# Spreading the last stores over two queues, reordering the last two chunks, and filling an early gap of VectorE, in an attention and mixture-of-experts kernel

## The chip, the cores and the metric

The kernel runs on one core of one Trainium2 chip. The metric is the device time of one execution in microseconds (us), taken as the median of several runs. The profile's span, from the first to the last instruction, is about 1.7 to 1.8 us shorter than the device time of the same run.

## The reference

Four batches and eight heads of causal attention (768 positions, 64 columns a head). Three of the eight heads see everything before them, the others only four first positions and a window of 64. The result, 3072 tokens of 512 columns, goes through eight experts whose gate weights are normalised eight times over rows and columns.

```python
def _moe_ref(x, w_gate, w1, w2):          # x: 3072 x 512 from the attention
    P = np.exp(logits - logits.max())     # logits = x @ w_gate, 8 experts
    for _ in range(8):
        P /= P.sum(1, keepdims=True) + 1e-09
        P /= P.sum(0, keepdims=True) + 1e-09
        P *= N / E
    out = np.zeros((N, D), dtype=np.float32)
    for e in range(E):
        h = np.maximum(x @ w1[e], 0.0)    # 512 -> 1024
        out += P[:, e:e + 1] * (h @ w2[e])  # 1024 -> 512
    return out
```

## The kernel before

The attention and the gate take the first 175 us. Then come 42 work items, seven experts times six chunks of 512 tokens. Each runs a first layer and a second layer, both with seven block products in place of eight, which needs sums and differences of blocks ("combinations") made on VectorE beforehand. The chunks' accumulators are named acc_79 to acc_84 in the profile. In the last expert each finished quarter of an accumulator is stored at once. The parts that matter (all else cut):

```python
works = [(e, c) for e in range(1, E) for c in range(NCH)]     # 7 experts x 6 chunks

def store(c, i, n):                       # a quarter of a chunk: two transfers of 128 KB
    for o in range(2):
        nc.sync.dma_start(                # all of them issued by SyncE
            out=out[ts(c, CH), :].rearrange(...)[i, n, o],
            in_=acc[c][64 * o:64 * o + 64, i, n, :, :])

def layer2(e, c):                         # 7 products: l2y, l2w, l2z in the profile
    ...
    for k in (1, 5, 6, 2, 7, 3, 4):
        bank, first, last, (i, n) = steps[k]
        product(k, bank, first, last)     # TensorE
        add(bank, i, n, by_dma=k in (...) and (e, c) not in works[-2:])
        ...                               # VectorE, or ScalarE and an accumulating DMA
        if e == E - 1 and done[i, n] == (1 if (i, n) == (1, 0) else 2):
            store(c, i, n)
        yield

def layer2_last(e, c):                    # the very last chunk: plain, "last" in the profile
    for q, i in ((0, 0), (0, 1), (1, 0), (1, 1)):
        ...                               # 8 matmuls of 512 columns, VectorE adds to acc
                for o in range(2):
                    (nc.scalar if o else nc.sync).dma_start(out=..., in_=acc[c][...])
                yield

# when VectorE makes which combination: (work item, slot) -> w2 ("w") or x ("x")
early = {(1, 1): "w", (1, 4): "xx", (2, 0): "w", (2, 1): "x", (2, 3): "w", (2, 4): "x",
         (3, 1): "wx", (3, 4): "x", (3, 5): "wx", (4, 1): "wx", (4, 5): "w"}

def body(n):
    ...
    if n == 0:
        run(gens["l1"], 9); run(combine_w1(1), 9); run(combine_x(0), 9)
        gens["w"], gens["x"] = combine_w2(1), combine_x(1)
        go("w")
        weigh_over()
    ...

with tc.manual_schedule(engines={mybir.EngineType.DVE}):      # VectorE's order is the program's
    for n in range(len(works)):
        body(n)
    go("h", 2)
    last = layer2_last(*works[-1])
    run(last, 1)                          # the last chunk's first block ...
    go("l2", 9)                           # ... then layer 2 of the chunk before it
    run(last, 9)
```

In this stage VectorE runs in program order. The orders of the other engines come from a scheduler.

The softmax here doesn't subtract the row's maximum and nothing guards it: scores larger than these inputs give would overflow.

Of the kernel before, what the change touches and what calls it, by code (L numbers as in the profile page):

```python
# [37 lines left out]
def kernel(  # L38
# [13 lines left out]
    nc = tc.nc  # L52
# [3 lines left out]
    E = moe_w_gate.shape[1]  # L56
# [93 lines left out]
    def load_w1(e):  # L150
        w1 = wp.tile([128, 4, FF], F16, tag="w1", name=f"w1_{e}")
        nc.gpsimd.dma_start(out=w1, in_=moe_w1[e].rearrange("(c p) f -> p c f", p=128))  # L152
        return w1

    def load_w2(e):
        w2 = wp.tile([128, 8, DM], F16, tag="w2", name=f"w2_{e}")
        nc.gpsimd.dma_start(out=w2, in_=moe_w2[e].rearrange("(c p) f -> p c f", p=128))
        return w2
# [246 lines left out]
    def run(g, n):  # L405
        for _ in range(n):
            if next(g, "end") == "end":
                return False
        return True
# [250 lines left out]
    def weigh_over():  # L660
        nc.vector.reciprocal(out=over0[:, :, 0], in_=Pne[:, :, 0])
        nc.vector.tensor_tensor(
            out=over0[:, :, 1:], in0=Pne[:, :, 1:LATE],
            in1=over0[:, :, 0:1].broadcast_to([128, NB, LATE - 1]), op=ALU.mult)
# [4 lines left out]
    def weight_first(c):  # L669


        wt = mp.tile([128, 4], F32, tag="wt", name=f"wt_{c}")

        def hold(i0, i1):
            nc.vector.tensor_copy(out=wt[:, i0:i1], in_=Pne[:, 4 * c + i0:4 * c + i1, 0])

        def weigh(i0, i1):
            for i in range(i0, i1):
                x = acc_of(4 * c + i)
                nc.scalar.activation(out=x, in_=x, func=AF.Copy, bias=0.0, scale=wt[:, i:i + 1])  # L680

        hold(0, 1)
        yield
        weigh(0, 1)
        yield
        hold(1, 4)
        yield
        weigh(1, 4)
        yield

    works = [(e, c) for e in range(1, E) for c in range(NCH)]
# [23 lines left out]
    def combine_w1(e):  # L715
        w1 = expw[e][0]
        X = mp.tile([128, 4, 2, 2, 256], F16, tag="S1", name=f"S1_{e}")
        w1 = w1.rearrange("p c (h i x) -> p c h i x", h=2, i=2)
        yield from left(lefts1, e, [[w1[:, 2 * k:2 * k + 2, :, i, :] for k in range(2)]
                                    for i in range(2)], [X[:, j] for j in range(4)])  # L720

    def combine_w2(e):
        w2 = expw[e][1]
        X = mp.tile([128, 4, 4, 256], F16, tag="T2", name=f"T2_{e}")
        yield from right(rights2, e, [[w2[:, 4 * k:4 * k + 4, ts(n, 256)] for n in range(2)]
                                      for k in range(2)], [X[:, j] for j in range(4)])

    def combine_w(e):
        yield from combine_w1(e)
        yield from combine_w2(e)  # L730

    def combine_x(d):
        X = mp.tile([128, 4, 2, 512], F16, tag=f"T1_{d}", bufs=1, name=f"T1_{d}")
        yield from right(rights1, d, [[xT[k][:, :, ts(2 * d + n, CH)] for n in range(2)]
                                      for k in range(2)], [X[:, j] for j in range(4)])

    def combine_h(e, c):
        h = [hTs[e, c, k].rearrange("p f (q i t) -> p i q f t", q=2, i=2) for k in range(2)]
        X = [mp.tile([128, 2, 4, 128], F16, tag=f"S2{j}", bufs=1, name=f"S2{j}_{e}_{c}")
             for j in range(4)]  # L740
        yield from left(lefts2, (e, c), [[h[k][:, i] for k in range(2)] for i in range(2)], X)
# [86 lines left out]

    def store(c, i, n):
        for o in range(2):  # L830
            nc.sync.dma_start(
                out=out[ts(c, CH), :].rearrange("(q i p c) (n d) -> i n c p q d", q=2, i=2, c=2, n=2)[i, n, o],
                in_=acc[c][64 * o:64 * o + 64, i, n, :, :],
            )

    def layer2(e, c):
# [39 lines left out]
        for k in (1, 5, 6, 2, 7, 3, 4):  # L876
            bank, first, last, (i, n) = steps[k]
            product(k, bank, first, last)
            add(bank, i, n, k in ((2, 3, 4, 7) if (e, c) in works[:2] else (2, 3, 4))
                and (e, c) not in works[-2:])  # L880
            done[i, n] = done.get((i, n), 0) + 1
# [4 lines that stand above are left out]
    def layer2_last(e, c):  # L886


        w2 = expw[e][1]
        for q, i in ((0, 0), (0, 1), (1, 0), (1, 1)):  # L890
            pieces = 1 + (q == 1 and i == 1)
            for n in range(pieces):
                width = 512 // pieces
                t = psB.tile([128, 512], F32, tag="l1" if n else "l2", name=f"last{q}{i}{n}")
                t = t[:, 0:width]
                for f in range(8):
                    nc.tensor.matmul(out=t, lhsT=hTs[e, c, f // 4][:, f % 4, ts(2 * q + i, 128)],  # L897
                                     rhs=w2[:, f, n * width:(n + 1) * width],
                                     start=(f == 0), stop=(f == 7))
                cols = slice(n, n + 1) if pieces == 2 else slice(0, 2)  # L900
                dst = acc[c][:, i, cols, q, :]
                nc.vector.scalar_tensor_tensor(
                    out=dst, in0=t.rearrange("p (n d) -> p n d", d=256),
                    scalar=Pne[:, 4 * c + 2 * q + i, e:e + 1], in1=dst, op0=ALU.mult, op1=ALU.add)
                rows = out[ts(c, CH), :].rearrange("(q i p c) (n d) -> q i c p n d", q=2, i=2, c=2, n=2)
                for o in range(2):
                    (nc.scalar if o else nc.sync).dma_start(
                        out=rows[q, i, o][:, cols], in_=acc[c][64 * o:64 * o + 64, i, cols, q, :])
                yield
# [7 lines left out]
    def go(name, n=1):  # L917
        run(gens[name], n)


    early = {(1, 1): "w", (1, 4): "xx", (2, 0): "w", (2, 1): "x", (2, 3): "w", (2, 4): "x",
             (3, 1): "wx", (3, 4): "x", (3, 5): "wx", (4, 1): "wx", (4, 5): "w"}

    def body(n):
        e, c = works[n]
        if c == 0 and e + 1 < E:
            w1s[e + 1] = load_w1(e + 1)
        if c == 1 and e + 1 < E:
            expw[e + 1] = w1s.pop(e + 1), load_w2(e + 1)
        if c == 2 and e + 1 < E:  # L930
            gens["w"] = chain(gens["w"], combine_w(e + 1))
        if e == LATE:
            gens["first"] = weight_first(c)
        if n == 0:
            run(gens["l1"], 9)
            run(combine_w1(1), 9)
            run(combine_x(0), 9)
            gens["w"], gens["x"] = combine_w2(1), combine_x(1)
            go("w")
            weigh_over()  # L940
        if n == 3:
            gens["x"] = combine_x(2)
        for slot in range(7):
            if slot in (1, 2):
                go("first")
            go("l1")
            if slot in (1, 2):
                go("first")
            for name in early.get((n, slot), ()) if n < 5 else ("w", "x") if slot in (1, 5) else ():
                go(name)  # L950
            go("l2")
            if slot in (2, 3):
                go("h")
        if n:
            gens["h"] = combine_h(*works[n - 1])
            go("h", 2)
            gens["l2"] = layer2(*works[n - 1])
        if n + 1 < len(works):
            e, c = works[n + 1]
            gens["l1"] = layer1(e, c // 2, c % 2)  # L960

    with tc.manual_schedule(engines={mybir.EngineType.DVE}):
        for n in range(len(works)):
            body(n)

        go("h", 2)
        last = layer2_last(*works[-1])
        run(last, 1)
        go("l2", 9)
        run(last, 9)  # L970
# [35 lines left out]
```

## Time and profile before

| | before |
|---|---|
| device time, three runs known at the prediction | 697.09 us (696.86 to 697.43) |
| span of the profiled run | 696.6 us |
| TensorE busy | 679.7 us, 98% |
| TensorE's last matmul ends / VectorE's last operation ends | 690.9 / 691.4 us |
| last issue of a store / its landing / span's end, after VectorE's end | 2.25 / 4.25 / 5.23 us |

TensorE is the limit nearly everywhere; only the two ends of the stage can give anything.

The chain of waits of before, its end (start, length, what):

```profile
679.69 0.74 DVE acc_84 L902
680.43 0.79 DVE acc_83 L862 x2
681.23 0.04 issue
681.27 1.03 PE l2y L845 x8
...
689.98 0.89 PE last_9348 L897 x8
690.87 0.02 issue
690.89 0.48 DVE acc_84 L902
```

TensorE waits for VectorE at 681.27, because VectorE first adds the last chunk's block (acc_84) and then chunk 4's (acc_83). From 681.27 on TensorE works through.

The timeline of SyncE of before (start, length, what, how many in a row) shows the queue of stores:

```profile
676.59 6.33 SPq L831 DMA_DIRECT2D out_dram<-acc_82  x5
683.01 0.59 SPq L907 DMA_DIRECT2D out_dram<-acc_84  x1
683.71 1.26 SPq L831 DMA_DIRECT2D out_dram<-acc_82  x2
685.07 6.43 SPq L831 DMA_DIRECT2D out_dram<-acc_83  x8
691.59 2.60 SPq L907 DMA_DIRECT2D out_dram<-acc_84  x4
```

One issue takes 0.6 us. The last chunk's four stores start at 691.59, after VectorE is done at 691.37, as the eight of acc_83 stand before them. The line's own statistics of before, in the same stretch (duration of one issue in ns: least, median, most; then the time from issue to landing):

```profile
L831 SPq DMA_DIRECT2D out_dram<-acc_83 x8: 596/600/1637, 685.1 to 690.9; - x8
...
DMA to landing us min/median/max: 2.4/2.9/4.6
```

The start of the expert stage: VectorE's timeline of before (in brackets the idle time before an operation and what ended it), and the waits of TensorE between 195 and 212.5 us.

```profile
181.83 0.20 DVE L662 TENSOR_TENSOR over_3012<-Pne,over_3012 128x24 f32<-128x24 f32 x1
184.10 0.69 DVE L795 CUSTOM_DVE_ANT_0 hT_3276<-l1z,R_3349 128x512 f16<-128x512 f32 x1 [2.07 <-ACT R_3349 L789]
184.71 0.68 DVE L710 TENSOR_TENSOR T_1_3340<-w_1_2268,T_1_3340 128x1024 f16<-128x1024 f16 x1
```

```profile
PE l1w L781 <- ACT R_3496 L789: 0.3, 1, 0.3
PE l2y L845 <- DVE S_1_0_3406 L701: 0.2, 1, 0.2
```

VectorE idles 2.07 us and soon after is so full that TensorE waits for it, directly (the second line) or through ScalarE (the first: before R_3496 ScalarE itself waits 3.1 us for VectorE's hT_3275).

### The profile page before, as it was taken

The numbers are of one execution on the slowest core, as the hardware profiler recorded it, in microseconds if no ns is written. First come the engines' busy times: TensorE is split into PE (matmuls) and PEld (weight loads), VectorE is DVE, ScalarE is ACT, GpSimd is POOL, SyncE is SP. The second block draws the span as 40 slices with busy tenths as digits, with TensorE's granted clock in tenths as the row PEclk, the third lists the DMA queues.
The fourth block names the chain that finished last, engine by engine and source line by source line (L and its number), as shares of the span: only waits on it lengthen the run. The fifth ranks groups of instructions, "written<-read, shape, count | busy, mean of one in ns | idle before, by whom it ended". The sixth has DMA issues, their size and how long they took to land.

```text
span 696.6 us, 14325 instructions
## 1 busy us (share of the span) xinstructions
PE 679.7 (98%) x5605; PEld 455.7 (65%) x5605; DVE 573.6 (82%) x1147; ACT 422.4 (61%) x779; POOL 159.8 (23%) x185
## 2 busy tenths in 40 slices
PE   6999999999999999999999999999999999999996
PEld 3566666766466666666666666666666666666664
DVE  7786776657799988998889789988998799887885
ACT  5787777774556677774655556565565646556550
POOL 7443330000022212121221212122122212212120
PEclk8999999999999999999999999999999999999999
DMA  9999692000634468337742764475645583434777
GB/s 178 178 183 146 44 84 14 1 2 5 117 61 76 77 109 137 58 67 131 121 78 54 129 98 90 73 120 84 107 77 91 89 133 62 76 57 91 158 142 191
DMA packets 102964, 65.96 MB, mean 95 GB/s; under 512 B 66800, under 2 KB 83184, under 8 KB 102896
## 3 DMA queue, kind: packets, MB, share of 16 engines
q0 software_dynamic: 93696, 57.69, 60.9%
q1 hardware_dynamic: 7552, 6.30, 3.7%
q10 hardware_dynamic: 1648, 1.05, 0.6%
q8 instruction: 44, 0.72, 0.4%
q14 instruction: 24, 0.20, 0.1%
HBM read 52.45 MB, written 6.29 MB: 84 GB/s over the span
## 4 chain that ended last, share of the span: by engine, by line
PE 88%; ACT 4%; DVE 4%; DMA 2%; issue 1%; ACTq 0%; DVEq 0%
PE l1y L781 20%; PE l2y L845 19%; PE l2w L845 10%; PE l1w L781 10%; PE l2z L845 5%; PE l1z L781 5%; DMA acc_82<-add 2%; PE l1b L762 1%; DMA ret_u<-in_is_retrieval_dram 1%; DVE acc_79 L862 0%; PE l_3153 L392 0%; PE l_3087 L392 0%; PE l_1496 L392 0%; ACT PT_1_0_0_302 L480 0%; PE last_9324 L897 0%
## 5 line engine op out<-in xcount | busy, mean ns | idle before, releaser
L859 ACT ACTIVATE add<-l2z,Pne 128x256 f32<-128x256 f32 x68 | 28.6, 471 | 75.5 <-PE l2z L845 75.5
L859 ACT ACTIVATE add<-l2w,Pne 128x256 f32<-128x256 f32 x68 | 28.6, 471 | 24.2 <-PE l2w L845 23.4
L378 PEld LDWEIGHTS <-w_0_124 128*128 128x128 f16 x384 | 35.5, 98 | 4.2 <-issue 0.4
L867 POOL DMA_DIRECT2D acc_79<-add x22 | 18.7, 849 | 84.6 <-ACT add L859 46.3
L859 ACT ACTIVATE add<-l2y,Pne 128x256 f32<-128x256 f32 x68 | 28.6, 471 | 10.5 <-PE l2y L845 9.1
L867 POOL DMA_DIRECT2D acc_80<-add x22 | 18.6, 846 | 64.7 <-ACT add L859 20.2
L867 POOL DMA_DIRECT2D acc_81<-add x21 | 17.7, 844 | 67.3 <-ACT add L859 24.6
L867 POOL DMA_DIRECT2D acc_82<-add x21 | 17.7, 845 | 63.5 <-DVE hT_3272 L795 24.4
L867 POOL DMA_DIRECT2D acc_83<-add x18 | 15.1, 837 | 58.9 <-ACT add L859 22.2
L867 POOL DMA_DIRECT2D acc_84<-add x18 | 15.4, 855 | 43.7 <-ACT add L859 34.1
L845 PEld LDWEIGHTS <-hT_3276 128*128 128x128 f16 x176 | 17.2, 98 | 6.7
L845 PEld LDWEIGHTS <-hT_3272 128*128 128x128 f16 x168 | 16.4, 98 | 6.6
L845 PEld LDWEIGHTS <-hT_3274 128*128 128x128 f16 x168 | 16.4, 98 | 6.2 <-issue 0.2
L845 PEld LDWEIGHTS <-hT_3273 128*128 128x128 f16 x160 | 15.6, 98 | 6.3
L845 PEld LDWEIGHTS <-hT_3277 128*128 128x128 f16 x160 | 15.7, 98 | 6.1
L845 PEld LDWEIGHTS <-hT_3275 128*128 128x128 f16 x152 | 14.9, 98 | 5.8
L862 DVE SCALAR_TENSOR_TENSOR acc_83<-l2y,Pne,acc_83 128x256 f32<-128x256 f32 x38 | 16.6, 478 | 1.9 <-PE l2y L845 1.8
L862 DVE SCALAR_TENSOR_TENSOR acc_79<-l2y,Pne,acc_79 128x256 f32<-128x256 f32 x36 | 15.7, 478 | 1.2 <-PE l2y L845 1.2
L862 DVE SCALAR_TENSOR_TENSOR acc_81<-l2y,Pne,acc_81 128x256 f32<-128x256 f32 x36 | 15.7, 478 | 1.2 <-PE l2y L845 1.2
L862 DVE SCALAR_TENSOR_TENSOR acc_80<-l2y,Pne,acc_80 128x256 f32<-128x256 f32 x36 | 15.7, 478 | 1.2 <-PE l2y L845 1.2
L862 DVE SCALAR_TENSOR_TENSOR acc_82<-l2y,Pne,acc_82 128x256 f32<-128x256 f32 x36 | 15.7, 478 | 1.2 <-PE l2y L845 1.2
L152 POOL DMA_DIRECT2D w_2_3280<-in_moe_w_dram x1 | 0.8, 759 | 69.2 <-PE l_3219 L378 69.2
(2421 smaller groups left out, 2203.1 us busy)
## 6 DMA issues: line engine op xcount, KB each, us to landing
acc_79<-add POOLq DMA_DIRECT2D x22, 256.0 KB, 3.2
acc_80<-add POOLq DMA_DIRECT2D x22, 256.0 KB, 3.2
acc_81<-add POOLq DMA_DIRECT2D x21, 256.0 KB, 3.2
acc_82<-add POOLq DMA_DIRECT2D x21, 256.0 KB, 3.3
acc_83<-add POOLq DMA_DIRECT2D x18, 256.0 KB, 3.2
acc_84<-add POOLq DMA_DIRECT2D x18, 256.0 KB, 10.2
w_0_124<-in_moe_w_dram POOLq DMA_DIRECT2D x1, 1024.0 KB, 11.7
w_0_131<-in_moe_w_dram POOLq DMA_DIRECT2D x1, 1024.0 KB, 18.2
```

The lines of the kernel that those rows point to most:

```text
L152: nc.gpsimd.dma_start(out=w1, in_=moe_w1[e].rearrange("(c p) f -> p c f", p=128))
L378: nc.tensor.matmul(out=l1[:, ts(fb % 2, 256)], lhsT=w1[:, dc, ts(fb, 128)], rhs=xT[dc // 2][:, dc % 2, c0:c0 + 256], start=(dc == 0), stop ...
L762: nc.tensor.matmul(out=l1, lhsT=w1[:, dc, ts(4 * half + f, 128)], rhs=xT[dc // 2][:, dc % 2, ts(2 * d + n, CH)], start=(dc == 0), stop=(dc ...
L781: nc.tensor.matmul(out=banks[g, bank], lhsT=lefts1[e][k - 1][:, dc, half, ts(g, 128)], rhs=rights1[d][k - 1][:, dc, :], start=(first and d ...
L845: nc.tensor.matmul(out=banks[bank][q], lhsT=lefts2[e, c][k - 1][:, q, f, :], rhs=rights2[e][k - 1][:, f, :], start=(first and q == 0 and f ...
L859: nc.scalar.activation(out=t[:, q, :], in_=banks[bank][q], func=AF.Copy, bias=0.0, scale=w)
L862: nc.vector.scalar_tensor_tensor(out=dst, in0=banks[bank][q], scalar=w, in1=dst, op0=ALU.mult, op1=ALU.add,)
L867: nc.gpsimd.dma_start(out=acc[c][:, i, n, :, :], in_=t, accum_op=ALU.add)
```

## The change

It has three parts. Part A takes half of the stores of the last but one chunk (acc_83) to ScalarE's queue, whose engine has no more to compute by then. Part B lets layer 2 of that chunk begin before the last chunk's first block. Part C moves three combinations of 0.6 to 0.7 us into VectorE's gap.

```diff
     def store(c, i, n):
         for o in range(2):
-            nc.sync.dma_start(
+            queue = nc.scalar if o and (E - 1, c) in works[-2:] else nc.sync    # A
+            queue.dma_start(
 ...
-    early = {(1, 1): "w", (1, 4): "xx", (2, 0): "w", (2, 1): "x", (2, 3): "w", (2, 4): "x",
+    early = {(1, 1): "x", (1, 4): "xx", (2, 3): "w",                            # C
              (3, 1): "wx", (3, 4): "x", (3, 5): "wx", (4, 1): "wx", (4, 5): "w"}
 ...
             go("w")
             weigh_over()
+            go("w", 2)                                                          # C
+            go("x")
 ...
         last = layer2_last(*works[-1])
+        go("l2")                                                                # B
         run(last, 1)
         go("l2", 9)
```

(The marks A, B and C are added here.)

## The prediction

> **What bounds it now.** TensorE: 98% busy on the page, and in the expert stage the timeline repeats every 12.15 us (28 matmuls of 512 columns at 0.216 us plus 56 of 256 at 0.108 us = 12.1 us), so the middle of the kernel offers nothing. Time can only come from two places, and the change touches just those.
>
> *The end.* By the timeline, TensorE's last matmul ends at 690.86, VectorE's last accumulation at 691.37, the span at 696.6. The 5.2 us between are stores. SyncE's queue is behind: one issue takes 0.60 us, about 0.65 from start to start; it issues acc_83's eight stores from 685.07 to 691.50 (the last four of them up to 4 us after their data) and only then the last chunk's four, at 691.59, 692.28, 692.98 and 693.63. The last lands at 695.63; the closing semaphores and drains take another 0.97. The ACT queue, empty of compute after 678.2, issues its last store at 692.08, landing at 694.44.
>
> *The start.* VectorE idles 2.07 us at 182.03 (waits view: hT_3276 waits for R), then works without a break from 191.78 to 204.1. In that stretch four combinations of w2 and x (0.6 to 0.7 us each) stand between the operations that TensorE waits for. Adding up matmul starts against their column counts, TensorE loses about 1.6 us from 184 to 212 above its usual pace; about 0.96 of that (at 195.23, 198.60, 199.91 and 211.95) lies after VectorE has become continuous.
>
> **What the change does.**
> 1. acc_83's stores: four on SyncE, four on ACT. SyncE loses 4 x 0.65 = 2.6 us of issue; its last store can then start when its data is there (about 0.1 us after VectorE's end) instead of 2.26 us later. The bytes and transfers are the same. The Trainium skill, "DMA: Bandwidth & Descriptors", section "Issuing engines are not separate DMA queues", says that issuing from several engines saves only the issue time; here exactly that is on the critical path, and the trace agrees (ACT's last store lands 1.2 us before SyncE's). With landing 2.0 to 2.4 us after issue: about -1.8 us.
> 2. Layer 2 of chunk 4 begins before the last chunk's first block. TensorE lost 0.39 us at 681.27 because VectorE did last_9219's accumulation (0.74 us) before the first l2y. Now l2y's accumulation comes first, but the second l2y's is then later and a new wait of about 0.3 us arises at the third. Net about -0.25 us.
> 3. Three combinations (3 x 0.65 = 1.95 us) move from the continuous stretch into the 2.07 us gap, which they just fill. Up to S_1_0's first combination (it waits for ScalarE's hT_3276 at 191.75) nothing changes; after it I expect most of the 0.96 us back: -0.8 us. As the rest is TensorE-bound, it survives to the end.
>
> All three lie on the critical path, one after the other.
>
> **Predicted: 697.09 - 2.85 = 694.2 us, range 693.2 to 695.5; faster by over 2%: 0.01; within 2%: 0.98; slower by over 2%: 0.01.**
>
> **Signs.** (1) From VectorE's last operation to the span's end 5.2 becomes about 3.4 us; SyncE's last issue within 0.8 us of VectorE's end. (2) The wait at the second l2y of the tail gone, one at the third. (3) The gap near 182 filled; the waits of TensorE between 195 and 212 mostly gone, the steady phase reached about 0.8 us earlier.
>
> **What would make it wrong.** Landings that take longer because the stores bunch (3 to 4 us happened at 684 and 688); an ACT or SyncE store held by the landing of an earlier one on the same semaphore; the chunk-3 stores (their accumulating transfer landed only at 683.6) holding SyncE still; the scheduler's new TensorE order putting new waits at the start.

## More of the kernel before

All runs told of here were with a mean granted TensorE clock of 0.990 to 1.000. The sessions of runs were on different chips. Each ratio compares a kernel with before on one chip and in the same rounds; two profiles can come from different chips.

The page of the profile of before starts with busy times and tells the DMA queues (packets, megabytes, share of 16 engines). Queue q1 is SyncE's stores, q10 ScalarE's.

```profile
PE 679.7 (98%) x5605; PEld 455.7 (65%) x5605; DVE 573.6 (82%) x1147; ACT 422.4 (61%) x779; POOL 159.8 (23%) x185
...
q1 hardware_dynamic: 7552, 6.30, 3.7%
q10 hardware_dynamic: 1648, 1.05, 0.6%
q8 instruction: 44, 0.72, 0.4%
```

## The result

| | before | after |
|---|---|---|
| device time, median of six runs | 696.57 us (695.88 to 697.43) | 695.66 us (695.23 to 697.86) |
| span of the profiled run | 696.6 us | 694.0 us |

The ratio after to before is 0.9992, with a 95% interval of 0.9976 to 1.0007. Ratios here are the mean time of one kernel's fast runs over that of the other's of the same rounds, so not quite the ratio of the medians. The predicted 694.2 us with its range of 693.2 to 695.5 was too low.

The spans alone would have looked like a triumph: 2.65 us less, when 2.85 was predicted. To see that this is misleading, I cut each span at four points that exist in every kernel: the first expert matmul, the 250th and the 3300th TensorE record after it, and the end of VectorE's last operation. These are my sums from the traces, in us:

```
                         before   before again  after   after again  after third
start to first matmul    175.88   174.52        174.98  174.13       175.62
to the 250th record       42.15    42.15         41.76   41.77        41.76
to the 3300th record     441.80   441.33        441.33  441.33       441.88
to VectorE's end          31.55    31.56         31.34   31.34        31.33
to the span's end          5.23     5.29          4.54    4.95         4.69
span                     696.61   694.85        693.95  693.51       695.27
```

The first row varies by up to 1.8 us in code that the change does not touch. The third had an extra 0.47 us in the profile of before and 0.55 us in the third of after: the same wait of TensorE for ScalarE near 399 us, absent in the other three. In these two profiles the accumulating transfer that ScalarE had waited for just before landed 12.0 and 12.1 us after its issue, in the other three after 10.9 to 11.1. The profile of before was a slow draw, and the record says so without a trace: the profiled execution took 698.31 us, while none of the six timed ones took over 697.43. What the change moved are rows two, four and five: -0.39, -0.22, and -0.3 to -0.7.

The page of the profile of after: TensorE's share and the queues.

```profile
PE 679.6 (98%) x5605; PEld 455.9 (66%) x5605; DVE 573.0 (83%) x1147; ACT 422.4 (61%) x779; POOL 159.6 (23%) x185
...
q1 hardware_dynamic: 6976, 5.78, 3.4%
q10 hardware_dynamic: 2224, 1.57, 0.8%
q8 instruction: 44, 0.72, 0.4%
```

0.52 MB, four transfers of 128 KB, went from q1 to q10, as meant. The tail of the chain of after:

```profile
680.16 0.88 DVE acc_83 L863 x2
681.04 0.04 issue
681.08 1.03 PE l2y L846 x8
...
688.01 0.89 PE last_9348 L898 x8
688.90 0.02 issue
688.92 0.48 DVE acc_84 L903
```

The old wait at the second l2y is gone and a shorter one, before the third, is there. From the spacing of matmul starts TensorE loses 0.39 us at the old place in before and 0.21 at the new one in after.

SyncE and ScalarE in after, by the timeline:

```profile
674.84 8.27 SPq L832 DMA_DIRECT2D out_dram<-acc_82  x7
683.21 0.60 SPq L908 DMA_DIRECT2D out_dram<-acc_84  x1
683.91 3.63 SPq L832 DMA_DIRECT2D out_dram<-acc_83  x4
688.42 2.68 SPq L908 DMA_DIRECT2D out_dram<-acc_84  x4
```

```profile
681.85 4.04 ACTq L832 DMA_DIRECT2D out_dram<-acc_83  x4
686.23 3.93 ACTq L908 DMA_DIRECT2D out_dram<-acc_84  x4
```

SyncE has only four stores of acc_83 now, and they end by 687.54. Yet it starts its last four at 688.42 and the very last at 690.46, 1.06 us after VectorE's end at 689.40. And there is another surprise: SyncE does all of acc_82's stores before the first one of acc_84, where before it did two of them after it. What SyncE waits for in after (for what, us in total, times, longest):

```profile
SPq L832 <- DMA acc_82<-add: 4.7, 3, 3.0
...
SPq L908 <- DMA out_dram<-acc_83: 0.8, 1, 0.8
...
SPq L832 <- DMA out_dram<-acc_84: 0.6, 1, 0.6
```

The last two are new: a store waits for the landing of an earlier store. The trace shows why: the stores use eight completion semaphores in turn, so each waits until the one eight before it has landed. The landings of the same stretch in after:

```profile
L832 ACTq DMA_DIRECT2D out_dram<-acc_83 x4: 602/602/634, 681.8 to 685.3; - x4
L832 SPq DMA_DIRECT2D out_dram<-acc_83 x4: 596/634/894, 683.9 to 686.9; - x4
...
DMA to landing us min/median/max: 2.4/3.4/4.5
```

The median rose from 2.9 to 3.4 us (for the stores of this line from 684.5 us on in before and from 683 us on in after, from 3.0 to 4.1). The longest, 4.6 and 4.5, belong to a store of acc_82 that both kernels issue 14 us before VectorE's end. Finally the start of the stage in after, VectorE's timeline:

```profile
180.93 0.20 DVE L662 TENSOR_TENSOR over_3012<-Pne,over_3012 128x24 f32<-128x24 f32 x1
181.04 0.68 DVE L710 TENSOR_TENSOR T_1_3340<-w_1_2268,T_1_3340 128x1024 f16<-128x1024 f16 x1
181.64 0.68 DVE L710 TENSOR_TENSOR T_1_3340<-w_1_2268 128x1024 f16<-128x1024 f16 x1
182.25 0.69 DVE L710 TENSOR_TENSOR T_1_3346<-xT_76 128x1024 f16<-128x1024 f16 x1
183.20 0.69 DVE L795 CUSTOM_DVE_ANT_0 hT_3276<-l1z,R_3353 128x512 f16<-128x512 f32 x1 [0.27 <-ACT R_3353 L789]
```

The gap is filled just as intended: 0.27 us are left of 2.07.

### The profile page after: what moved, and what is told of

Read it like the earlier page. It is cut to its first block, busy times and chain, and to the rows that moved or that the text cites. A ratio compares the mean times of both kernels' runs of the same rounds, so it can differ in the third digit from the quotient of the medians.

```text
span 694.0 us, 14330 instructions
## 1 busy us (share of the span) xinstructions
PE 679.6 (98%) x5605; PEld 455.9 (66%) x5605; DVE 573.0 (83%) x1147; ACT 422.4 (61%) x779; POOL 159.6 (23%) x185
## 4 chain that ended last, share of the span: by engine, by line
PE 92%; ACT 3%; DVE 3%; issue 1%; DMA 1%; DVEq 0%; ACTq 0%
PE l1y L781 20%; PE l2y L846 20%; PE l1w L781 10%; PE l2w L846 10%; PE l1z L781 5%; PE l2z L846 5%; PE l1b L762 1%; DMA ret_u<-in_is_retrieval_dram 1%; DVE acc_83 L863 0%; PE l_3153 L392 0%; PE l_3087 L392 0%; PE l_1496 L392 0%; ACT PT_1_0_0_302 L480 0%; PE last_9312 L898 0%; PE l_3069 L392 0%
```

## The experiments

Seventeen runs were made; e1, e2 and e15 repeat the two kernels unchanged. The quotes below call the theories by letters. A is the first theory: the two traces' stretches show the true sizes (start -0.4, tail -0.2, stores less than predicted, as part B changes SyncE's order), and the rest of the difference of the spans is chance; its rival is that the prediction's sizes hold. D is the theory that the stores in flight simply delay one another. The letters differ from those of the change's parts. F puts the slow landings down to an instruction read of 16 KB, and G a longer closing down to a pause of SyncE at a fixed place of its program. All numbers "after D" in the quotes and below are counted from the end of VectorE's last operation, D.

This table holds the end of every profile: last issue, last landing and span's end after D, and "closing", the time from the last landing to the end.

| run | last issue | last landing | closing | end |
|---|---|---|---|---|
| before | 2.25 | 4.25 | 0.98 | 5.23 |
| e1, before again | 2.31 | 4.31 | 0.97 | 5.29 |
| after | 1.06 | 3.14 | 1.40 | 4.54 |
| e2, after again | 1.54 | 3.52 | 1.43 | 4.95 |
| e15, after a third time | 1.21 | 3.28 | 1.41 | 4.69 |
| e3, A alone | 0.23 | 2.57 | 1.41 | 3.98 |
| e4, C alone | 2.92 | 4.92 | 0.97 | 5.89 |
| e5, B alone | 2.02 | 4.02 | 0.97 | 4.99 |
| e6, A and C | 0.18 | 2.70 | 1.48 | 4.18 |
| e7, after, first block by ScalarE | 0.91 | 3.17 | 1.51 | 4.68 |
| e8, after, half the bytes | 0.18 | 2.51 | 1.48 | 3.99 |
| e9, after, shifted | 0.47 | 2.69 | 1.41 | 4.10 |
| e10, A and C, shifted | 0.25 | 2.79 | 1.48 | 4.26 |
| e11, e7 shifted | 0.17 | 2.42 | 1.55 | 3.97 |
| e12, before, shifted | 1.84 | 3.84 | 0.98 | 4.82 |
| e13, after, more SyncE transfers | 0.60 | 2.87 | 1.10 | 3.98 |
| e14, e11, more SyncE transfers | 0.20 | 2.78 | 1.03 | 3.81 |
| e16, e11, later transfers | 0.25 | 3.19 | 1.04 | 4.23 |
| e17, after, later transfers | 1.01 | 3.05 | 1.11 | 4.16 |

### Repeats: e1, e2 and e15

No edit: the kernel before and the kernel after, run again.

> The kernel before, unchanged, against itself. It tells how far a single profile can be trusted. If the profile of before (span 696.6 us) was a slow draw, this one ends earlier (694.5 to 696), first scores near 9.0 us instead of 9.98, and the wait of 0.47 us at 399.8 may be gone; if that profile was typical, first scores again at about 10.0 and span again 696.6. Ratio to before 1.000 within 0.001 either way.

> The changed kernel, unchanged, with more rounds. Theory A (each part is worth less than predicted: stores 0.7, layer 2 first 0.2, combinations 0.4): ratio 0.9981 (-1.3 us). Rival B (the prediction was right and the timed runs were unlucky): ratio 0.9959 (-2.85 us). Rival C (nothing real, the two profiles differ by chance): 1.000.

> The changed kernel again, on the chip and in the rounds of the two others, for a direct comparison and a third profile of its end: ratio 0.998, 4.5 to 5 us from VectorE's end.

Measured with five rounds each: e1 0.9995 (0.9983 to 1.0008), which shows the noise of the method; e2 0.9981 (0.9967 to 0.9994), 695.79 against 697.25 us; e15 0.9983 (0.9971 to 0.9996), 696.10 against 697.35. In these two comparisons the change saves about 1.3 us, just resolved, half of what was predicted; the first comparison, whose interval includes 1, did not resolve it. The spans are in the table above: e1's is 694.85, so 1.8 us of the span of the first profile of before were chance. As expected of a slow draw, e1's first scores came at 8.89 us instead of 9.98, and the wait near 399 us was gone.

### The parts alone: e3, e4, e5, e6

e3 has part A only, e4 part C only, e5 part B only, and e6 parts A and C without B:

```diff
 # e6 = after, but
         last = layer2_last(*works[-1])
-        go("l2")
         run(last, 1)
```

> Only the stores of chunks 4 and 5 by two queues. Theory A: from VectorE's last operation to the span's end 5.2 becomes 4.5 us, because stores that meet in time land later (over 4 us) and hold the next store on the same completion semaphore; ratio 0.999 (-0.7 us). The prediction's term: 3.4 us and -1.8 us, ratio 0.9974.

> Only the three combinations moved into VectorE's gap. Theory A: about 0.96 us of TensorE's waits between 195 and 212 go, but new ones of 0.18, 0.18 and 0.11 us come (at the y and w accumulations of the second work), so -0.4 us, ratio 0.9994. The prediction's term: -0.8 us, ratio 0.9989.

> Only layer 2 of chunk 4 begun before the last chunk's first block. Theory A (what this part earns on TensorE, 0.22 us, it loses at the stores, because on SyncE the last chunk's first store now stands behind chunk 3's last two, which wait for an accumulating transfer): from VectorE's end to the span's end not 5.2 to 5.3 but 5.3 to 6 us, ratio 1.000. The prediction's term: VectorE ends 0.25 us earlier, the stores as before, ratio 0.9996.

> The change without its layer-2 part. Theory A: from VectorE's end to the end about 4.0 us as with the stores alone (4.5 and 4.9 in the changed kernel's two profiles), the start 0.39 us shorter: -1.65 us, ratio 0.9976, at least as fast as the changed kernel. If the layer-2 part is a gain as predicted: 0.2 us slower than the changed kernel.

| run | ratio to before (95%) | median, before's | first 250 records | 3300th record to D |
|---|---|---|---|---|
| e3, A | 0.9980 (0.9968 to 0.9993) | 695.56, 697.25 | 42.15 | 31.55 |
| e4, C | 0.9994 (0.9981 to 1.0006) | 696.37, 697.25 | 41.76 | 31.56 |
| e5, B | 1.0000 (0.9988 to 1.0013) | 697.27, 697.28 | 42.15 | 31.34 |
| e6, A and C | 0.9975 (0.9963 to 0.9988) | 695.39, 697.28 | 41.75 | 31.55 |

Each TensorE term belongs to one part: C gives 0.39 us at the start and B 0.22 in the tail, to 0.01 us the same with and without the others. Part A alone takes the end from 5.3 to 3.98 us after D, 1.3 us, as much as the whole change; with B beside it (after, e2, e15) the end is at 4.5 to 4.95. So B gives TensorE 0.2 us and, by these profiles, costs the stores 0.6 to 1.0 (0.4 to 0.8 against e6, which has C as after has). The timed runs do not resolve this cost: e6's 0.9975 and the 0.9981 and 0.9983 of after have intervals that overlap. SyncE's timeline of e3 shows the order that it keeps without B: the last two stores of acc_82 behind the first one of acc_84, and only 0.33 us between acc_83's stores and the last four, where after has 0.88.

```profile
674.82 6.33 SPq L832 DMA_DIRECT2D out_dram<-acc  x5
681.25 0.60 SPq L908 DMA_DIRECT2D out_dram<-acc  x1
681.95 4.14 SPq L832 DMA_DIRECT2D out_dram<-acc  x6
686.42 3.95 SPq L908 DMA_DIRECT2D out_dram<-acc  x4
```

Misses: e5 ended 4.99 after D where theory A wanted 5.3 to 6, so B does not hurt the stores by itself. e4's end of 5.89, where its stores are those of before (5.23 and 5.29), shows that this stretch varies by itself, too. Theory A missed e3 as well: it wanted 4.5 and a ratio of 0.999, as stores that meet would hold the end even without B. Nor was e3's 3.98 the 3.4 of the prediction, although its last issue (0.23) and the landing (2.34 later) were just as predicted. The missing 0.4 us is in the closing, 1.41 where 0.97 was taken for granted.

### SyncE's order: e7

With part B the scheduler puts the first block of acc_84 behind all of acc_82 in SyncE's queue, and the last two of acc_82 wait for accumulating transfers that land 7.6 us before D. In after the DMA engines' busy share falls to 0.42 in the stretch from 7 to 6 us before D; in before and e3 it is 0.8 and more. e7 takes that block off SyncE.

```diff
-                    (nc.scalar if o else nc.sync).dma_start(
+                    (nc.scalar if o or (q, i) == (0, 0) else nc.sync).dma_start(
```

> The changed kernel with both first stores of the last chunk on the ACT queue, so that none stands behind chunk 3's waiting stores on SyncE. Theory A (the order on SyncE is what spoils the end): DMA busy without the dip to 0.4 seven us before VectorE's end, 3.9 to 4.2 us from VectorE's end to the span's end, ratio 0.9973 (-1.9 us). Rival D (the transfers themselves, bunched by two queues, are the limit whatever their order): 4.5 to 4.9 us as in the changed kernel.

Measured: 0.9971 (0.9958 to 0.9985), 695.49 against 697.28 us, five rounds. The dip of the DMA engines went (0.94 in that stretch), but the end came 4.68 us after D, not the 3.9 to 4.2 of theory A. The order is not what delays the last stores, at least not alone. Theory A is too short.

### Fewer bytes: e8

If the stores slow each other down by their bytes, half the bytes must cure it. This kernel leaves half of the stored blocks unwritten and so gives a wrong result.

```diff
-                out=...[i, n, o],
-                in_=acc[c][64 * o:64 * o + 64, i, n, :, :],
+                out=...[i, n, o][:, :, 0:128],
+                in_=acc[c][64 * o:64 * o + 64, i, n, :, 0:128],
```

> The changed kernel, its stores of chunks 0 to 4 with half the bytes each (128 of 256 columns; the result is wrong on purpose), as many stores and descriptors, in the same order. If the DMA engines' throughput holds the end (they are 0.9 to 1.0 busy from 9 us before VectorE's end): landings of 2 to 3 us instead of 4.2 to 4.5, no store held by an earlier landing, 3.2 to 3.6 us from VectorE's end to the span's end. If the sequencers' issue time holds it: no change, 4.5 to 4.9 us.

Measured with three rounds: 0.9971 (0.9957 to 0.9985), end at 3.99 after D, not 3.2 to 3.6. Most stores landed within 2.1 to 2.8 us, yet some still needed 4. The landings of e8's halved stores of acc_83 that were issued from about 6 us before D on:

```profile
DMA to landing us min/median/max: 2.1/3.5/4.1
```

This failure told most. A list of the stores in question from the trace, my reading (times from D):

```
queue   issued   landed   took
SyncE    -5.92    -3.83   2.09
ScalarE  -5.56    -1.44   4.12
SyncE    -5.23    -1.23   4.00
SyncE    -4.35    -1.02   3.33
ScalarE  -4.35    -0.81   3.54
SyncE    -3.18    -0.61   2.57
```

A transfer's semaphore is raised 16 times. For the first two slow stores 15 of the 16 raises came by -3.47 and -3.17 and the 16th at -1.44 and -1.23. The Trainium skill, "DMA: Bandwidth & Descriptors", section "Why a DMA increments its semaphore by 16 and not by 1", says that the engines finish independently and that only the full 16 means that all data has landed. The trace agrees, and it says more here: all but one of the shares had landed, and the last was 2 us behind. At -3.50 a packet of 16 KB of the queue that the page lists as "q8 instruction" starts, and takes 0.88 us. Which DMA engine carries it, and so whether it is the one behind, the records that I read do not tell.

The page of after has 44 such packets with 0.72 MB. The Trainium skill, "Runtime: NRT & Kernel Launch", section "Instruction fetch mechanics", states that an engine's instruction memory is refilled in blocks of 16 KiB, 256 instructions, by DMA. The trace agrees: TensorE has 2 x 5605 = 11,210 records of matmuls and weight loads, and 11,210 / 256 = 43.8. In the traces of before and after the last of these reads starts 4.31 and 3.16 us before D (it takes 1.25 and 0.88 us), among the stores. This is theory F: the stores in flight land late because of that read, and the stores that use their semaphores next wait.

### Moving the instruction read: e9 to e12

If the read goes by TensorE's instruction count, more instructions at the start bring it forward. Nine warming matmuls of 512 columns became six, with 32 short ones added, 29 more in all, or 58 records:

```diff
-        keep_warm(blank[:, 0:128], blank, 9)
+        keep_warm(blank[:, 0:128], blank, 6)
+        keep_warm(blank[:, 0:128], blank[:, 0:16], 32)
```

e9 does it to after, e10 to e6 (A and C), e11 to e7, e12 to before.

> The changed kernel with 29 more matmuls in TensorE's idle time before the first transpose (6 of 512 columns and 32 of 16 in place of 9 of 512), so that the 16 KB instruction read on one DMA engine, which every profile has 3.2 to 4.5 us before VectorE's end (once per 256 rows of TensorE), comes some 4 us earlier, at -7 to -9. Theory F (that read holds up one of the 16 DMA engines, the stores then in flight land 4 us after issue, and the next store on the same completion semaphore waits): stores issued after -6 land in 2.2 to 3 us, no store waits for an earlier one, 3.5 to 4.0 us from VectorE's end to the span's end instead of 4.5 and 4.9. Rival D (too many bytes at once): landings of 4 us stay at -6 to -4, 4.5 to 4.9 us.

> The same shift for the change without its layer-2 part. Theory F: a little better than its 4.0 to 4.2 us from VectorE's end, 3.5 to 4.0. Rival D: 4.0 to 4.2 as before.

> The same shift for the changed kernel with both first stores of the last chunk on the ACT queue. Theory F: 3.5 to 4.0 us instead of 4.7 and so the fastest of all, ratio about 0.997 or less. Rival D: 4.7 us.

> The same shift for the kernel before. Theory F: SyncE's issue of 1.64 to 1.71 us at -4.3 becomes 0.6 and the stores issued from -6 on land in under 3 us; SyncE's eleven issues of 0.65 us from -6.3 on still set the end, so 4.2 to 4.8 us from VectorE's end to the span's end instead of 5.2 to 5.3: part of what the change gained is then had without it. Rival D: 5.2 to 5.3.

| run | last 16 KB read, before D: unshifted, shifted | end after D: unshifted, shifted | ratio to before (95%) | median (before: 697.23) |
|---|---|---|---|---|
| e9 (after) | 3.16 (e2: 3.47), 6.42 | 4.54 to 4.95, 4.10 | 0.9977 (0.9964 to 0.9989) | 695.71 |
| e10 (A and C) | 3.47, 6.03 | 4.18, 4.26 | 0.9974 (0.9961 to 0.9987) | 695.53 |
| e11 (e7) | 3.62, 6.07 | 4.68, 3.97 | 0.9972 (0.9960 to 0.9985) | 695.39 |
| e12 (before) | 4.31, 6.82 | 5.23 and 5.29, 4.82 | 1.0002 (0.9983 to 1.0021) | 696.80 |

(e12 with three rounds, the others with five.) The read moved by about 2.5 to 3.3 us (to -6.0 to -6.8, where -7 to -9 was expected), TensorE's own rows of the stretch table stayed within 0.01 us of those of the unshifted kernels (the chance wait near 399 us apart), and the slow landings moved with the read: in e12 the stores issued at -5.24 to -3.20 landed after 2.39 to 2.51 us, where before's at -5.66 to -4.31 took 3.4 to 3.8 us; those issued at -8.38 to -7.04 took 3.2 to 3.9 us, where before's took 2.4 to 2.5. In before one issue of SyncE at -4.31, the moment of the read, lasted 1.64 us; in e12 the issues of that time last 0.6 us. The statistics of the stores of e12 over the same stretch as before's:

```profile
L832 SPq DMA_DIRECT2D out_dram<-acc x14: 595/598/1040, 675.4 to 688.3; - x14
...
DMA to landing us min/median/max: 2.4/2.8/4.6
```

The longest issue is 1.04 now, and it lies at -6.33, beside the moved read at -6.82. The longest landing, 4.6 as in before, is again the store issued 14 us before D, far from either read.

What follows the read is a late sixteenth share, and the traces hold far more of it than the tail. In all 19 of them together, 704 output stores had no read of "q8 instruction" running between their issue and their fifteenth raise, and not one of these had its sixteenth raise over 0.5 us behind the fifteenth. Of the 246 stores with such a read, 122 had. With the moved reads of e9 to e12 this shows that the read can hold up one share of a store in flight. A slow landing alone is not the sign: 155 of the 704 took over 3.3 us too, with all shares late together, like the two issued 14 us before D in before and after (4.4 to 4.6 us). For those theory D stays open. The chance wait near 399 us fits the picture: the sixteenth share of its accumulating transfer was 2.2 us (before) and 2.0 us (e15) behind the fifteenth, with a read running, and 0.6 to 1.1 us in e1, after and e2. Why the read delays what is in flight by some 2 us in e8, against the 0.9 us that it takes itself, is not explained.

For the end of the kernel it matters where its stores are held by semaphores: the shift takes 0.4 to 0.9 us in after, 0.7 in e7 and 0.4 to 0.5 in before, and nothing in e6. These are single profiles, and the timed runs do not resolve a gain from the shift: 0.9977 beside 0.9981 and 0.9983 for after, 0.9972 beside 0.9971 for e7, 1.0002 for before. F expected a gain for e10 too and missed, and e9 lies 0.1 above its range; the ends of e11 and e12 came as expected (e12 at the upper bound), but e11 was not the fastest of all as F wanted. F also wanted no store to wait and landings of 2.2 to 3 us after -6 in e9; several still waited there for an earlier one (those issued at -4.23, -3.38 and -2.94 among them), and landings took up to 3.5 us. That the read does no harm in e6 and e3 looks like luck of turn: the next store of SyncE, at -3.2, uses a semaphore whose earlier store had landed at -3.75 or -3.78, just before the read. In after the same semaphore's store was one of those held up, and landed at -1.05; the next store on it left at -0.99. This pairing is read from the traces; that it is the cause of B's cost is an inference that fits after, e2, e3, e6, e9 and e11. With the read moved, the kernels with B end at 4.10 and 3.97, no later than e10 without it (4.26).

### The closing: e13, e14, e16, e17

At the end SyncE waits for the semaphores of all stores, one by one. In all runs up to e12 with part A the closing lasts 1.40 to 1.55 us, in those without it 0.97 or 0.98. In nine traces checked SyncE pauses for 0.41 to 0.44 us once, always after the 79th of its records (of 89 without part A, of 85 with it, of 91 and 93 in e13 and e17). My reading of both ends (times from D):

```
before: wait for the 4th semaphore at 3.18, next instruction at 3.62; last landing 4.25
after:  wait for the 8th semaphore at 3.16, next instruction at 3.60; last landing 3.14
```

In before the pause falls in a time when SyncE waits anyway. With four stores fewer in its queue it falls after the last landing. That is theory G; the rival was that the last landings bunch. Four tiny transfers put onto SyncE (and as many onto ScalarE, so that the turn of the semaphores stays) earlier on must bring the pause forward again, and the closing back to 1.0:

```diff
+        if n in (20, 21, 22, 23):
+            for queue in (nc.sync, nc.scalar):
+                queue.dma_start(out=<a spare tile>, in_=<the retrieval flags>)      # e13, e14
+                queue.dma_start(out=<a spare tile>, in_=<a copy made by VectorE>)   # e16, e17
```

(One of the two lines in each kernel; e13 and e17 start from after, e14 and e16 from e11.)

> The changed kernel with four more tiny loads on SyncE (and four on ACT, so that the completion semaphores fall as before), issued in the third expert, far from both ends. Theory G: from the last landing to the span's end 0.97 us instead of 1.40 to 1.43, everything else as in the changed kernel, so 4.1 to 4.5 us from VectorE's end. Rival H: 1.40 stays.

> All repairs together: first stores of the last chunk on ACT, the instruction read of TensorE moved earlier, four SyncE transfers more. Theory G: 3.4 to 3.6 us from VectorE's end to the span's end (3.97 without the last), ratio 0.9965. Rival H: 4.0.

> As e14, with the eight tiny transfers (a 128x8 copy of the weights inside the SBUF) tied to a copy made in the third and fourth expert. Start as always (first expert matmul at 174 to 176 us), 3.5 to 3.9 us from VectorE's end to the span's end of which 1.0 to 1.1 after the last landing, ratio 0.9965 (-2.4 us).

> As e13, with the transfers tied in the same way. 4.0 to 4.4 us from VectorE's end to the span's end, 1.0 to 1.1 after the last landing instead of 1.40, ratio 0.9977.

Measured, five rounds each: closings of 1.10, 1.03, 1.04 and 1.11 us, as G said. In e17 the pause is at 1.55 to 1.99 us after D, ahead of the last landing at 3.05. So G is shown, as to where the 0.4 us came from. As versions they failed. In e13 and e14 the tiny loads depended on nothing, so the scheduler issued them at 1.9 to 8.9 us, among the kernel's first loads, and the first expert matmul came at 181.6 and 182.4 us: ratios 1.0065 (1.0051 to 1.0079) and 1.0066 (1.0053 to 1.0079), 702.05 and 701.82 against 697.35 us. e16 and e17 made the loads depend on a late value. That mended the start, but the middle took 442.13 and 441.81 us instead of 441.33, by new waits of TensorE near 422, 447 and (e16) 472 us and not by the chance wait near 399, which eats the gain: 0.9981 (0.9968 to 0.9995) and 0.9992 (0.9979 to 1.0004), 696.10 and 695.93 against 697.02; both missed the ratio that was expected (0.9965 and 0.9977). Of the expected ends only e17's came: e13's 3.98 is below its range, e14's 3.81 and e16's 4.23 are above theirs.

Why SyncE pauses was not tested. In nine traces checked an 8 KB read of the queue "q14 instruction" starts 0.6 to 0.9 us after the pause's end, so it may be the crossing into another block of SyncE's own instructions.

No version was shown to beat the changed kernel. e6, e7, e10 and e11, at 0.9971 to 0.9975 of before, have intervals that overlap with its 0.9981 and 0.9983.

## Why the prediction was wrong, point by point

- **The base.** "697.09" held: before measured 696.57 to 697.35 in the sessions. But its profile was a slow draw, 1.8 us longer than the repeat, so spans could be compared only stretch by stretch.
- **Step 1, the stores, "about -1.8 us": the step that failed.** The sum behind it was last issue at about 0.1, landing 2.0 to 2.4, closing 0.97, in all about 3.4 us after VectorE's end. Measured in after: 1.06 + 2.08 + 1.40 = 4.54. The landing was right. The closing was 0.43 too short, as taking four stores off SyncE moved its fixed pause from a time of waiting to the end (e13, e14, e16 and e17). The last issue, by the prediction's words "its last store can then start when its data is there (about 0.1 us after VectorE's end)", was put about 1 us too early (1.06, 1.54 and 1.21 measured): a store also waits for the landing of the store eight before it on its semaphore, and those landings took up to 4.5 us around an instruction read. With the read moved, the last issue came at 0.47 (e9) and 0.17 (e11, with e7's edit). What part of the slow landings is the read and what part bunching was not separated. The step was worth -0.3 to -0.7 in the three profiles of after, and -1.3 alone (e3). The list of what could go wrong named bunched landings and "an ACT or SyncE store held by the landing of an earlier one on the same semaphore"; the second happened, and got no weight in the sum or the range.
- **Citing "Issuing engines are not separate DMA queues".** The skill's sentence, that more issuing engines save only the issue time, holds: e3's last issue came 2.1 us earlier. "Here exactly that is on the critical path" was true for before. Once it was gone, semaphores and closing came next, and they were not in the sum.
- **Step 2, layer 2 ahead, "net about -0.25 us".** TensorE gained 0.22, with the new wait at the third l2y as foreseen. What was missed is that SyncE's order comes from the scheduler and changes with it; beside it the end of step 1 came 0.4 to 1.0 us later in the profiles. The order of that one block alone is not the cause, as e7 still ended at 4.68; the pairing of semaphores with the read is the inference above. By the profiles, the two steps were not additive.
- **Step 3, the combinations, "-0.8 us".** The gap filled as foreseen, but the gain was 0.39, to 0.01 us the same in all kernels with part C. The four waits named, 0.96 us, did go; new ones of 0.18, 0.18 and 0.22 us arose at 198.7, 200.1 and 210.5 (the traces name ScalarE's copies R, twice, and VectorE's hT). "I expect most of the 0.96 us back" was the mis-sized term: here the busy stretch gave back 0.39 us of the 0.96 that it showed as waits, as other waits took their place.
- **Sum.** -0.39 - 0.22 - 0.3 to -0.7 is -0.9 to -1.3 us; the medians gave -0.9, and the repeats with five rounds -1.46 (e2) and -1.25 (e15).

## What to carry to other kernels

When you shorten a queue at the end of a kernel, write down what will be the next limit and its size: the landing of the transfer that used the semaphore before, and what the engine does between the last landing and the end. Ahead of that, cut two profiles of the same kernel at fixed points, to learn which stretches vary by themselves; a difference of spans can be mostly chance. Two changes that both touch an order made by a scheduler should be tried apart before their gains are added.

## What the Trainium skill lacked or had wrong

- "Runtime: NRT & Kernel Launch", section "Instruction fetch mechanics", calls the cost of crossing an instruction block mostly hidden. For TensorE itself no run here shows otherwise. But transfers in flight are touched, which the page does not say: with a refill of 16 KB (0.88 to 1.35 us for the last one of each profile) under way, 122 of 246 stores had their sixteenth share over 0.5 us, and up to 2.6 us, behind the fifteenth, without one none of 704; 29 more matmuls moved the refill and the late shares with it.
- No page says that SyncE can pause for 0.41 to 0.44 us at a fixed place of its program (seen in before, after and seven more traces), and that this can lengthen the time from the last landing to the end, here from 0.97 us to between 1.40 and 1.55.
- "DMA: Bandwidth & Descriptors", section "Issuing engines are not separate DMA queues", calls the issue time usually small relative to the transfer. Here it was 0.60 us against 2.4 to 2.9 us for an undisturbed store of 128 KB, and taking four issues out of a row of them was worth 1.3 us at the end (e3).
- No page tells how far equal code varies: the first 175 us of this kernel took 174.1 to 175.9 us in the profiles without tiny loads.
